# An attention-and-MLP kernel: feed-forward over four stages at once in its second half, and one order list for the whole program

## The chip, the core and the metric

The kernel runs on one core of a Trainium2 chip. The metric is device time in microseconds (us) of one execution; the median of several runs is given.

## The reference

A linear attention with decay over `r`, `k`, `v` of 4 batches, 8 heads, 768 tokens and 48 channels, then a feed-forward layer over all 3072 tokens of 384 channels:

```python
for t in range(S):
    cur = np.einsum('bhd,bhe->bhde', u[None] * kt, vt)
    y[:, :, t] = np.einsum('bhd,bhde->bhe', rt, state + cur)
    state = w[None, :, :, None] * state + np.einsum('bhd,bhe->bhde', kt, vt)
...
x = attn_out.transpose(0, 2, 1, 3).reshape(B * S, H * D)     # 3072 x 384
h = x @ w_in                                                 # 384 x 2048
g = np.maximum(0.01 * h, h)
return g @ w_out                                             # 2048 x 384, float32
```

## The kernel before

The work is cut into 24 stages of 128 tokens of one batch; stage n is chunk n // 4 of batch n % 4, so that the state that stage n leaves is wanted by stage n + 4. Inside a stage the recurrence is turned into matrix products. Everything is kept in bf16, with sums in PSUM, which has eight banks that are taken and given back in the order of the program.

What a stage needs, with the letters by which the order list names each step (the number behind the letter is the stage):

- `r`, `k`, `v`: its three loads, issued by GpSimd (line 220; 128 x 8 runs of 192 bytes each, cast to bf16 on the way). `wi`, `wo`: a quarter of `w_in` and of `w_out` (lines 230 and 234), four of each, also GpSimd's.
- `P`: VectorE multiplies r (`Pnq`) or k (`Pnk`) by a table of decay powers into `qk` (line 361). `T` and `t`: TensorE transposes the one or the other and ScalarE (with `@` VectorE) copies it out to `tp`, in stages 0 to 5; from stage 6 on `XnT`, a DMA transpose issued by SyncE (line 366), does it. For stage 0 the raw r and k are cast (`c0q`, `c0k`, ScalarE), transposed, and multiplied by the tables on VectorE (`t0q`, `t0k`); `E` makes these tables with four exponentials on ScalarE.
- `A`: eight small matmuls of 48 rows on TensorE (`a_mm`, line 453), q against k within the chunk, into two banks. `M`: VectorE masks each of the two (`Mna`, `Mnb`; line 462, from stage 4 on a predicated copy, line 466) into `at`.
- The term in u: in stages 0 to 3 `X`, `D`, `Q` (a product on VectorE, four small matmuls, a scaling of v on VectorE). From stage 4 on `q` (`row_sums`): three VectorE instructions, `ku` (line 390), `rku` (line 392) and a reduction (line 394), and `Q` (`diag_tile`): two GpSimd multiplies (line 401) that lay these sums on the diagonal of `at`, before the masks are copied over it.
- `Y`: 16 or 28 matmuls on strips of 32 columns of TensorE's array (`y_mm`, line 592), `y`: ScalarE copies the result to `xT`.
- `K`: four matmuls for the state (`kv_mm`, line 494), `S`: VectorE folds them in (`state`; an add from PSUM, line 560, and a multiply by the decay, line 562; one instruction in stages 0 to 3).
- The feed-forward layer: `G` and `g`, first product for one stage and four blocks of 128 hidden channels (12 matmuls of 128 columns, line 631) and its leaky ReLU on ScalarE into `gT`; `J` and `j`, the same for a pair of stages and two blocks (6 matmuls of 256 columns, line 654). `H` and `h`: second product of one stage (16 matmuls of 384 columns, line 678), its copy on ScalarE and its store from SyncE's queue.
- `F`: fillings, matmuls of ones by ones whose result nobody reads (line 267). `v0z` and `v0y` zero the gap columns of `v_sb` for stages 0 to 3 and 4 to 23 (line 285). `utab`, `qtab`, `ktab`, `Cu`, `Cw`, `Wl`, `W`, `C`: small tables.

Each engine carries out its instructions strictly in the order in which the program lists them; a scheduler class adds the semaphores. Up to stage 5 of the feed-forward part (and up to stage 7 of the attention) the order is the list `ORDER`, written out by name. From there a loop over pairs m = 3 to 11 takes over: eight `g1_pair` with the `a_mm` of the next pair between or behind them, masks, preparation (`prep`, `row_sums`, `diag_tile`) of the pair after that, loads two pairs further, and around `y_part`, `kv_mm` and `state` the two `g2` of the pair before. These loads are paced: each waits until TensorE has done the second `g1_pair` of its m. `xT` and `gT` have three buffers of two stages.

Of the kernel before, what the change touches and what calls it, by code (L numbers as in the profile page):

```python
# [26 lines left out]
ORDER = """
w8 k0 r0 u8 u v0z v0 ones table v0y tcol trow r2 tri id wlz id8 k2 zr F18 Cw c0k Wl wi1 F4 T0k qk0 E r5 c0q F10 T0q wu8
k1 F1 TQ t0k r1 TK t0q qtab Cu ktab P2q v2 F3 A0 X0 W C P2k T2q k3 M0a D0 T2k t2q Q0 v1 t2k M0b F16 A2 r3 X2 Y0 P1k M2a
wi3 D2 y0 T1k P1q M2b v3 t1k F3 T1q K2 u16 Q2 G0.1 k5 S2 t1q Y2 g0.1 P3k k4 X1 A1 y2 P5q K1 P3q D1 T3k wi2 M1a T5q t3k  # L30
T3q U t5q@ r4 t3q G2.1 Q1 utab A3 wi0 X3 g2.1 G0.3 M1b wo0 M3b D3 K3 g0.3 Y1 v5 M3a G2.3 y1 Q3 k6 G1.3 P4k g2.3 q5 k7
Y3 g1.3 T4k y3 v4 G1.1 t4k S3 G3.2 wo1 g1.1 P4q P5k G3.1 Q5 g3.2 S1 T5k g3.1 T4q G3.3 q4 t4q G0.0 t5k r6 g3.3 A4 A5
g0.0 P0k G3.0 Q4 M5a K0 G1.2 g3.0 M5b S0 K5 G2.2 g1.2 wo3 G2.0 M4a g2.2 wo2 P7k G1.0 g2.0 P6k M4b r7 K4 Y5 g1.0 S4 Y4
r9 y5 G0.2 S5 y4 k9 J2.7 g0.2 q6 r8 J2.5 j2.7 J2.6 k8 j2.5 J2.4 P6q j2.6 Q6 J2.0 X6T j2.4 J2.1 j2.0 J2.2 j2.1 k10 H2
j2.2 P7q q7 v6 X7T v7 P9q v8 H3 P9k h2 q9 X9T Q7 P8q H1 h3 Q9 q8 v9 P8k A6 h1 X8T A7 M6b H0 Q8 M6a M7b M7a v11 K7 Y6 h0
r10 S7 Y7 y6 K6 k11 y7 J2.3 S6 v10 j2.3 r11
"""
# [89 lines left out]
def bass_rwkv5_eagle__then__act_leaky_relu_kernel(  # L127
# [317 lines left out]
    def a_mm(n):  # L445
        it = n % NTP
        at_bank[n] = (take(), take())

        def emit():
            for p in range(NP):  # L450
                for hh in range(2):
                    rows = slice(64 * hh, 64 * hh + D)
                    last = PE.matmul(at_bank[n][hh][0][:, 128 * p:128 * p + 128], tp[it][rows, NP + p, :],  # L453
                                     tp[it][rows, p, :], start=True, stop=True)
# [167 lines left out]
    def g1(n, grp):
        ps_g, key = g_bank[n, grp] = take()
        m, half = divmod(n, 2)
        ix, t = m % NX, slice(128 * half, 128 * half + 128)
# [9 lines left out]
        add("pe", emit, R=[("xT", ix, half), ("win", grp)], W=[key, ("pace", n, grp)])

    def g1_out(n, grp):
        ps_g, key = g_bank[n, grp]
        m, half = divmod(n, 2)
        ig, t = m % NG, slice(128 * half, 128 * half + 128)  # L640
        add("act", lambda: A.activation(gT[ig][:, 4 * grp:4 * grp + 4, t],  # L641
                                        ps_g[:, :].rearrange("p (f t) -> p f t", t=128), AF.Prelu, alpha=0.01),
            R=[key], W=[("gT", ig, half, 2 * grp), ("gT", ig, half, 2 * grp + 1)])
        give(key)

    def g1_pair(m, j):
        ps_g, key = g_bank[m, j, 2] = take()
        ix = m % NX

        def emit():  # L650
            for f in range(2):
                fb = 2 * j + f
                for s in range(NSL):
                    last = PE.matmul(ps_g[:, 256 * f:256 * f + 256], w_in_sb[:, s, 128 * fb:128 * fb + 128],  # L654
                                     xT[ix][:, s, :], start=s == 0, stop=s == NSL - 1)
            return last

        add("pe", emit, R=[("xT", ix, 0), ("xT", ix, 1), ("win", j // 2)],
            W=[key, ("pace", 2 * m, j), ("pace", 2 * m + 1, j)])

    def g1_pair_out(m, j):
        ps_g, key = g_bank[m, j, 2]
        ig = m % NG
        add("act", lambda: A.activation(gT[ig][:, 2 * j:2 * j + 2, :].rearrange("p f t -> p (f t)"),  # L664
                                        ps_g[:, :], AF.Prelu, alpha=0.01),
            R=[key], W=[("gT", ig, 0, j), ("gT", ig, 1, j)])
# [4 lines left out]
    def g2(n, c0=0, c1=HD):
        ps_o, key = o_bank[n, c0] = take()
        m, half = divmod(n, 2)
        ig = m % NG

        def emit():
            for s in range(NFB):
                last = PE.matmul(ps_o[:, 0:c1 - c0], gT[ig][:, s, 128 * half:128 * half + 128], w_out_sb[:, s, c0:c1],  # L678
                                 start=s == 0, stop=s == NFB - 1)
# [47 lines left out]
    for name in ORDER.split():  # L727
        if name in single:
            single[name]()
        else:  # L730
            what, n, rest = re.match(r"([A-Za-z]+?)(\d+)(.*)$", name).groups()
            stage[what](int(n), rest)
    for m in range(FIRST // 2, NST // 2):
        due, ahead, far = ([n for n in (2 * m + x, 2 * m + x + 1) if n < NST] for x in (2, 4, 6))
        late = m < FIRST // 2 + LATE
        for j in range(8):
            if j == VISIT and not late:
                for n in due:
                    a_mm(n)
            g1_pair(m, j)  # L740
            g1_pair_out(m, j)
        for n in due if late else ():
            a_mm(n)
        if not late:
            for n in ahead:
                prep(n)
        for n in due:
            a_mask(n)
        if late:
            for n in ahead:  # L750
                prep(n)
        for n in far:
            load_stage(n, pace=[("pace", 2 * m, 1)])
        for n in ahead:
            row_sums(n)
            diag_tile(n)
        g2(2 * m - 2)
        g2_out(2 * m - 2)
        for n in due:
            y_part(n)  # L760
        turning = [n for n in due if n < NST - NB]
        for n in turning:
            kv_mm(n)
        for n in turning:
            state(n)
        g2(2 * m - 1)
        g2_out(2 * m - 1)
    g2(NST - 2)
    g2_out(NST - 2)
# [60 lines left out]
```

## Time and profile before

| what | us |
|---|---|
| median of 3 runs | 169.99 (169.92 to 170.53) |
| the profiled execution | 170.09 |
| its span in the profile | 168.3 |
| TensorE matmuls busy in the span | 161.6 |
| VectorE busy | 110.2 |
| GpSimd busy | 111.1 |
| ScalarE busy | 91.0 |

Busy times are sums over the span. The granted TensorE clock is 1.00 in every 10 us of the span but the last, where it is 0.99. In listings of groups the columns are line, engine, operation, output and inputs, shape, count, then busy us and mean ns of one, then the idle time just before and what ended it. PE is TensorE, PEld its weight loads, DVE VectorE, ACT ScalarE, POOL GpSimd, SP SyncE.

### The profile page before, as it was taken

What the parts mean: (1) busy time and instruction counts of PE and PEld (TensorE: products, weight loads), DVE (VectorE), ACT (ScalarE), POOL (GpSimd) and SP (SyncE); (2) the same over time, 40 slices, a digit from 0 to 9 for tenths busy, and PEclk for the clock granted to TensorE, in tenths of its full rate; (3) what the DMA queues carried; (4) which work ended last, traced back from release to release, by engine and by line L of the source; (5) the groups of instructions that cost most, each with busy time, mean ns of one, the idle gap of its engine ahead of it and who ended that gap; (6) DMA issues with size and microseconds to landing.
All of it is one profiled execution on the core that took longest, in us unless ns stands there. A gap on an engine that the chain in (4) does not pass through costs nothing.

```text
span 168.3 us, 4915 instructions
## 1 busy us (share of the span) xinstructions
PE 161.6 (96%) x2116; PEld 122.6 (73%) x2116; DVE 110.2 (66%) x221; ACT 91.0 (54%) x168; POOL 111.1 (66%) x125
## 2 busy tenths in 40 slices
PE   5889979999999999999999999999999999999994
PEld 5767869986568768768668768768678678668663
DVE  7499978828992497497599998996996805000000
ACT  4658777892228537537436536537537447449221
POOL 7999996999699929939939976975960540000000
PEclk9999999999999999999999999999999999999999
DMA  7999999999999996995994995994999111011012
GB/s 108 105 157 162 171 192 167 150 170 155 150 230 150 118 95 186 80 126 156 90 147 129 125 162 142 153 97 113 146 104 143 32 47 51 0 51 47 29 65 95
DMA packets 101263, 20.18 MB, mean 120 GB/s; under 512 B 94457, under 2 KB 101242, under 8 KB 101242
## 3 DMA queue, kind: packets, MB, share of 16 engines
q0 software_dynamic: 76512, 10.03, 93.3%
q1 hardware_dynamic: 23690, 9.64, 28.1%
q8 instruction: 16, 0.26, 0.7%
q10 hardware_dynamic: 1040, 0.20, 0.6%
q14 instruction: 5, 0.04, 0.1%
HBM read 20.45 MB, written 4.72 MB: 150 GB/s over the span
## 4 chain that ended last, share of the span: by engine, by line
PE 69%; POOL 12%; DMA 9%; DVE 7%; issue 1%; ACT 0%; POOLq 0%; DVEq 0%
PE ps L678 31%; PE ps L654 29%; DMA k_sb<-in_k_dram 5%; PE ps L592 5%; DMA r_sb<-in_r_dram 4%; POOL r_sb L220 3%; DVE qk L361 3%; PE ps L453 3%; POOL k_sb L220 3%; POOL v_sb L220 2%; PE ps L494 2%; DVE at L466 1%; POOL at L401 1%; POOL w_in_sb L230 1%; DVE rku L392 1%; DVE ku L390 1%
## 5 line engine op out<-in xcount | busy, mean ns | idle before, releaser
L678 PE MATMUL ps<-w_out_sb,gT 128*128 128x384 bf16 (+2 forms) x400 | 65.6, 320 | 0.0
L401 POOL TENSOR_TENSOR at<-ident,s_tok 128x512 bf16<-128x512 bf16 x40 | 42.8, 1101 | 21.0 <-DVE s_tok L394 21.0
L654 PE MATMUL ps<-xT,w_in_sb 128*128 128x256 bf16 x480 | 54.9, 273 | 0.0
L678 PEld LDWEIGHTS ps<-w_out_sb,gT 128*128 128x128 bf16 x400 | 37.7, 98 | 22.4
L664 ACT ACTIVATE gT<-ps 128x512 bf16<-128x512 f32 x80 | 47.8, 597 | 8.7 <-PE ps L654 4.0
L654 PEld LDWEIGHTS ps<-xT,w_in_sb 128*128 128x128 bf16 x480 | 46.4, 98 | 6.7
L690 ACT ACTIVATE out_sb<-ps 128x384 f32<-128x384 f32 (+2 forms) x25 | 12.0, 479 | 55.8 <-PE ps L678 55.8
L466 DVE CAST_PREDICATED at<-mask,ps 128x512 bf16<-128x512 uint16 x40 | 25.0, 684 | 21.8 <-PE ps L453 21.8
L220 POOL DMA_DIRECT2D k_sb<-in_k_dram x23 | 21.1, 923 | 3.3 <-PE ps L654 3.3
L220 POOL DMA_DIRECT2D v_sb<-in_v_dram x24 | 22.2, 925 | 0.8 <-POOLq L815 0.8
L220 POOL DMA_DIRECT2D r_sb<-in_r_dram x23 | 21.0, 914 | 0.0
L392 DVE TENSOR_TENSOR rku<-r_sb,ku 128x384 bf16<-128x384 bf16 x20 | 17.8, 892 | 0.7
L631 PE MATMUL ps<-xT,w_in_sb 128*128 128x128 bf16 x192 | 12.6, 219 | 0.5 <-DMA w_in_sb<-in_moe_w_in_dram 0.5
L606 ACT ACTIVATE xT<-ps 128x384 bf16<-128x384 f32 x24 | 10.9, 491 | 2.3 <-PE ps L592 2.2
L361 DVE TENSOR_TENSOR qk<-r_sb,qtab 128x384 bf16<-128x384 bf16 x23 | 9.1, 400 | 4.5 <-DMA r_sb<-in_r_dram 4.1
L631 PEld LDWEIGHTS ps<-xT,w_in_sb 128*128 128x128 bf16 x192 | 10.9, 98 | 1.3 <-DMA w_in_sb<-in_moe_w_in_dram 0.7
L394 DVE TENSOR_REDUCE s_tok<-rku 128x8 f32<-128x384 bf16 x20 | 11.1, 553 | 0.7
L641 ACT ACTIVATE gT<-ps 128x512 bf16<-128x512 f32 x16 | 9.5, 599 | 3.4 <-PE ps L631 2.9
L562 DVE TENSOR_TENSOR st<-sum_t,wl 128x384 bf16<-128x384 bf16 x16 | 10.7, 672 | 0.5
L592 PE MATMUL ps<-at,v_sb 128*32 128x128 bf16 x384 | 10.7, 219 | 0.0
L361 DVE TENSOR_TENSOR qk<-k_sb,ktab 128x384 bf16<-128x384 bf16 x23 | 9.9, 434 | 0.7 <-DMA k_sb<-in_k_dram 0.7
L592 PEld LDWEIGHTS ps<-tp,st 128*32 128x32 bf16 x240 | 7.2, 96 | 3.1 <-issue 2.5
(64 smaller groups left out, 120.9 us busy)
## 6 DMA issues: line engine op xcount, KB each, us to landing
out_dram<-out_sb SPq DMA_DIRECT2D x23, 192.0 KB, 2.2
v_sb<-in_v_dram POOLq DMA_DIRECT2D x24, 96.0 KB, 5.3
r_sb<-in_r_dram POOLq DMA_DIRECT2D x23, 96.0 KB, 5.4
k_sb<-in_k_dram POOLq DMA_DIRECT2D x23, 96.0 KB, 5.1
w_in_sb<-in_moe_w_in_dram POOLq DMA_DIRECT2D x4, 384.0 KB, 7.0
w_out_sb<-in_moe_w_out_dram POOLq DMA_DIRECT2D x4, 384.0 KB, 8.5
tp<-qk SPq DMA_TRANSPOSE x18, 4.1
k_f<-in_k_dram ACTq DMA_DIRECT2D x1, 192.0 KB, 2.8
```

The costliest lines, as they stand in the source:

```text
L220: add("pool", lambda: G.dma_start(dst, src), R=pace, W=[(which, n)], dma=f"{which}{n}")
L361: add("dve", lambda: V.tensor_tensor(qk[iq][:, H * half:H * half + H, 0:D], hd(src), hd(tab[:, :]), ALU.mult), R=[(name, n), "qk"[half] + ...
L392: add("dve", lambda: V.tensor_tensor(rku[i2][:, :], r_of(n), ku[i2][:, :], ALU.mult), R=[("r", n), ("ku", i2)], W=[("rku", i2)])
L394: add("dve", lambda: V.tensor_reduce(s_tok[i2][:, :], hd(rku[i2][:, :]), AX.X, ALU.add), R=[("rku", i2)], W=[("s", i2)])
L401: add("pool", lambda hh=hh, s_of=s_of: G.tensor_tensor(at[ia][:, hh, :, :], ident[:, :].unsqueeze(1).to_broadcast([128, NP, 128]), s_of.un ...
L466: add("dve", lambda: V.copy_predicated(at[n % NAT][:, hh, :, :], mask[:, :].bitcast(mybir.dt.uint16).unsqueeze(1).to_broadcast([128, NP, 1 ...
L592: last = PE.matmul(ps_y[32 * q:32 * q + 32, 128 * s:128 * s + 128], a, m, start=not whole and step == 0, stop=step == len(columns[q]) - 1)
L631: last = PE.matmul(ps_g[:, 128 * f:128 * f + 128], w_in_sb[:, s, 128 * fb:128 * fb + 128], xT[ix][:, s, t], start=s == 0, stop=s == NSL - 1)
L654: last = PE.matmul(ps_g[:, 256 * f:256 * f + 256], w_in_sb[:, s, 128 * fb:128 * fb + 128], xT[ix][:, s, :], start=s == 0, stop=s == NSL - 1)
L664: add("act", lambda: A.activation(gT[ig][:, 2 * j:2 * j + 2, :].rearrange("p f t -> p (f t)"), ps_g[:, :], AF.Prelu, alpha=0.01), R=[key], ...
L678: last = PE.matmul(ps_o[:, 0:c1 - c0], gT[ig][:, s, 128 * half:128 * half + 128], w_out_sb[:, s, c0:c1], start=s == 0, stop=s == NFB - 1)
L690: add("act", lambda: A.activation(out_sb[io][:, c0:c1], ps_o[:, 0:c1 - c0], AF.Copy), R=[key], W=held)
```

## The change

From stage 12 on, the first product is done for four stages and one block of hidden channels at a time: `Z` and `z`, three matmuls of 512 columns and one copy of 128 x 512. One function `g1_wide` with its width stands for `G`, `J` and `Z`. `xT` and `gT` become two buffers of four stages. The loop over pairs is gone; the list names every step of all 24 stages but the last `H`, which is still done in two halves behind it. No load waits for a place of TensorE any more: GpSimd issues each as it comes to it in the list. Fillings are F10, F20 and F2, 32 matmuls, where there were F18, F4, F10, F1, F3, F16 and F3, 55 matmuls.

```diff
-FIRST, NB, PACE = 6, B, 3
-TURNED, DIAG, CARRY, EXACT, RAW, VISIT, LATE = 6, 4, 4, 1, 1, 3, 3
+NB = B
+TURNED, DIAG, CARRY, EXACT, RAW = 6, 4, 4, 1, 1
 ORDER = """
-w8 k0 r0 u8 u v0z v0 ones table v0y tcol trow r2 tri id wlz id8 k2 zr F18 Cw c0k Wl wi1 F4 T0k qk0 E r5 c0q F10 T0q wu8
-k1 F1 TQ t0k r1 TK t0q qtab Cu ktab P2q v2 F3 A0 X0 W C P2k T2q k3 M0a D0 T2k t2q Q0 v1 t2k M0b F16 A2 r3 X2 Y0 P1k M2a
...
+w8 trow k0 table ones wlz wi1 r0 zr u v0z F10 tcol id u8 id8 tri c0k r2 k2 c0q r3 k1 qk0 wu8 Cw Wl r1 E F20 T0q t0q T0k
+t0k W TQ qtab P2q TK ktab k3 Cu C v0 P2k A0 M0a T2q u16 t2q P3q v2 X0 v3 wi3 P1k k4 M0b P1q v1 T2k U t2k T3q k5 utab
+T1k t1k X2 A2 P3k r4 r5 D0 M2a Q0 T1q t1q wi2 t3q T3k t3k F2 A1 D2 M2b Y0 wi0 y0 A3 K2 Q2 Y2 M1b G0.1 wo2 X3 D3 v4 X1
+D1 y2 v5 M3a G2.1 g2.1 M3b G0.3 Q3 Y3 y3 M1a G2.3 Q1 Y1 y1 g2.3 wo3 g0.3 G3.3 g3.3 P0k S2 P4k K0 G1.1 wo0 g0.1 r7 q5 k7
+T4k t4k G3.1 P5k T5k g1.1 K1 S0 q4 G3.2 g3.2 t5k wo1 G0.2 S1 G1.3 Q4 P4q g0.2 T4q t4q P5q T5q Q5 v0y k6 t5q@ g1.3 G2.2
+r6 G0.0 k9 g2.2 A4 r9 A5 G1.0 g3.1 M4a M4b k8 g1.0 M5a K3 G1.2 K5 r10 g1.2 v6 k10 G3.0 g3.0 Y4 y4 M5b Y5 G2.0 y5 J2.6
+J2.0 g0.0 g2.0 J2.3 J2.1 j2.1 J2.4 S5 P7k J2.7 j2.4 j2.7 j2.6 r8 S3 v7 P7q j2.3 j2.0 q7 v8 Q7 K4 S4 J2.2 j2.2 J2.5 P6k
+k11 X7T v9 H3 P6q q6 Q6 r11 H1 r13 H0 P8k k12 q9 Q9 r12 A7 j2.5 P9k k14 r15 X6T h0 A6 M6b M6a P9q X9T M7a H2 K7 Y6 v12
+y6 M7b Y7 r14 y7 H4 J3.1 P8q X8T q10 q8 J3.6 k13 h4 h3 P10k h1 J3.2 h2 q11 j3.2 J3.7 j3.1 k15 S7 K6 S6 J3.4 J3.0 j3.6
+j3.7 A9 M9b v11 A8 J3.3 j3.3 K8 P11k S8 H5 Q8 v10 M8a M8b Y8 y8 Q11 M9a Y9 y9 J3.5 J4.0 j4.0 P11q X11T j3.4 j3.0 J4.4
+j3.5 j4.4 k17 J4.3 j4.3 P12k J4.6 P10q X10T q12 h5 J4.7 v13 P12q P13q P13k J4.2 q13 K9 Q10 q14 K12 j4.2 r16 X13T j4.7
+Q14 J4.5 j4.5 S12 P14q Q13 K11 P15k Q12 P15q S11 J4.1 S9 X12T H6 q15 Q15 A10 P14k A11 M11a j4.1 H7 X14T v15 M11b M10b
+j4.6 K13 k19 X15T v14 M10a Y11 y11 Y10 y10 h6 A13 M13b r22 M13a H8 P16q h7 h8 k23 A14 M14a A12 M12b A15 H9 M12a M14b
+K10 M15a J5.5 j5.5 S10 M15b J5.6 Y14 y14 Y12 Y15 P19k r17 q17 Y13 y15 J5.4 v17 v16 J5.0 y12 y13 Z3.14 k16 K14 j5.6 J5.3
+P17q S13 j5.4 P16k J5.7 S14 Z3.9 P17k r19 X17T K17 Z3.0 P19q j5.3 X19T r21 k18 P21q j5.7 r18 P18k z3.14 Z3.15 z3.9 v18
+q16 k21 v19 j5.0 Z3.13 z3.13 P18q Q16 K18 S18 J5.2 j5.2 z3.15 Z3.8 Z3.7 k20 q18 K15 X16T z3.8 P21k K16 Z3.11 S16 Q17
+q19 Q19 h9 J5.1 Z3.1 Z3.12 r20 j5.1 H10 X21T z3.7 z3.12 z3.11 A17 z3.0 q21 S17 M17a S15 A16 M16a Z3.2 z3.2 H11 M16b
+z3.1 M17b X18T v22 k22 A18 Q18 h10 A19 M18a Q21 M18b A21 Z3.10 Z3.6 z3.10 M19a Y16 P22q y16 r23 Y18 M19b y18 Y17 Y19
+y17 P20q v20 K19 S19 y19 Z3.4 v23 z3.4 Z3.3 z3.3 Z4.9 Z3.5 z3.6 Z4.8 z4.8 z4.9 Z4.12 q22 Q22 Z4.1 Z4.7 z3.5 P23q q23
+M21b v21 Z4.11 h11 Z4.15 P22k P20k X20T Z4.5 z4.15 q20 Z4.10 H14 X22T P23k X23T z4.12 Z4.2 M21a z4.1 z4.7 z4.10 Z4.3
+z4.5 z4.2 H13 z4.3 A23 Q23 A20 h14 A22 z4.11 M23a M23b M22a Z4.4 H12 Q20 M20b M20a Y20 Y21 M22b h12 Y22 y22 Y23 y23 H15
+z4.4 y21 y20 Z5.12 Z5.1 z5.1 Z5.7 Z5.2 Z5.0 Z4.13 z5.0 Z5.5 h15 z5.5 Z5.13 Z5.15 z4.13 z5.2 z5.7 Z4.14 z5.15 Z4.0 z4.0
+z4.14 Z5.11 z5.13 Z5.8 Z4.6 z4.6 h13 Z5.10 Z5.3 H18 z5.10 z5.12 Z5.6 z5.6 H16 Z5.9 h16 z5.3 h18 z5.11 Z5.4 H17 h17 z5.8
+Z5.14 z5.14 H19 z5.9 z5.4 H21 H20 h20 H22 h19 h22 h21
 """
...
-    NQK, NTP, NVS, NAT, NT, NX, NG, NO = 6, 6, 6, 6, 10, 3, 3, 4
+    NQK, NTP, NVS, NAT, NT, NX, NG, NO = 6, 6, 6, 6, 10, 2, 2, 4
...
-    xT = [SB(f"xT{i}", [128, NSL, 256]) for i in range(NX)]
-    gT = [SB(f"gT{i}", [128, NFB, 256]) for i in range(NG)]
+    xT = [SB(f"xT{i}", [128, NSL, 512]) for i in range(NX)]
+    gT = [SB(f"gT{i}", [128, NFB, 512]) for i in range(NG)]
...
+    def g1_wide(n0, width, fb0, count):
+        ps_g, key = g_bank[n0, width, fb0] = take()
+        ix, slots = n0 // 4 % NX, range(n0 % 4, n0 % 4 + width)
+        t, step = slice(128 * slots[0], 128 * slots[0] + 128 * width), 128 * width
+
+        def emit():
+            for f in range(count):
+                fb = fb0 + f
                 for s in range(NSL):
+                    last = PE.matmul(ps_g[:, step * f:step * f + step], w_in_sb[:, s, 128 * fb:128 * fb + 128],
                                      xT[ix][:, s, t], start=s == 0, stop=s == NSL - 1)
             return last
...
+        "G": lambda n, x: g1_wide(n, 1, 4 * int(x[1:]), 4), "g": lambda n, x: g1_wide_out(n, 1, 4 * int(x[1:]), 4),
+        "J": lambda n, x: g1_wide(2 * n, 2, 2 * int(x[1:]), 2), "j": lambda n, x: g1_wide_out(2 * n, 2, 2 * int(x[1:]), 2),
+        "Z": lambda n, x: g1_wide(4 * n, 4, int(x[1:]), 1), "z": lambda n, x: g1_wide_out(4 * n, 4, int(x[1:]), 1),
...
-        "L": lambda n, x: load_stage(n, pace=[("pace", PACE, 0)]),
+        "L": lambda n, x: load_stage(n),
...
-    for m in range(FIRST // 2, NST // 2):
...
+    run(ORDER)
```

More of the change, by code (lines that the diff above doesn't have):

```diff
@@ L23 @@
 NSL = HD // 128
-FIRST, NB, PACE = 6, B, 3
-TURNED, DIAG, CARRY, EXACT, RAW, VISIT, LATE = 6, 4, 4, 1, 1, 3, 3
+NB = B
+TURNED, DIAG, CARRY, EXACT, RAW = 6, 4, 4, 1, 1
 ORDER = """
-w8 k0 r0 u8 u v0z v0 ones table v0y tcol trow r2 tri id wlz id8 k2 zr F18 Cw c0k Wl wi1 F4 T0k qk0 E r5 c0q F10 T0q wu8
-k1 F1 TQ t0k r1 TK t0q qtab Cu ktab P2q v2 F3 A0 X0 W C P2k T2q k3 M0a D0 T2k t2q Q0 v1 t2k M0b F16 A2 r3 X2 Y0 P1k M2a
-wi3 D2 y0 T1k P1q M2b v3 t1k F3 T1q K2 u16 Q2 G0.1 k5 S2 t1q Y2 g0.1 P3k k4 X1 A1 y2 P5q K1 P3q D1 T3k wi2 M1a T5q t3k
@@ L31 @@
[L31 to L35, printed above, removed]
@@ L36 @@
-r10 S7 Y7 y6 K6 k11 y7 J2.3 S6 v10 j2.3 r11
+w8 trow k0 table ones wlz wi1 r0 zr u v0z F10 tcol id u8 id8 tri c0k r2 k2 c0q r3 k1 qk0 wu8 Cw Wl r1 E F20 T0q t0q T0k
+t0k W TQ qtab P2q TK ktab k3 Cu C v0 P2k A0 M0a T2q u16 t2q P3q v2 X0 v3 wi3 P1k k4 M0b P1q v1 T2k U t2k T3q k5 utab
+T1k t1k X2 A2 P3k r4 r5 D0 M2a Q0 T1q t1q wi2 t3q T3k t3k F2 A1 D2 M2b Y0 wi0 y0 A3 K2 Q2 Y2 M1b G0.1 wo2 X3 D3 v4 X1
+D1 y2 v5 M3a G2.1 g2.1 M3b G0.3 Q3 Y3 y3 M1a G2.3 Q1 Y1 y1 g2.3 wo3 g0.3 G3.3 g3.3 P0k S2 P4k K0 G1.1 wo0 g0.1 r7 q5 k7
@@ L604, in y_out @@
         ps_y, key = y_bank[n]
-        m, half = divmod(n, 2)
-        add("act", lambda: A.activation(xT[m % NX][:, :, 128 * half:128 * half + 128],
+        ix, slot = n // 4 % NX, n % 4
+        add("act", lambda: A.activation(xT[ix][:, :, 128 * slot:128 * slot + 128],
                                         ps_y[:, 0:HD].rearrange("p (s t) -> p s t", t=128), AF.Copy),
-            R=[key], W=[("xT", m % NX, half)])
+            R=[key], W=[("xT", ix, slot)])
         give(key)
@@ L620, in bass_rwkv5_eagle__then__act_leaky_relu_kernel @@
     g_bank = {}
[L622 to L625, printed above, removed]
+    def g1_wide(n0, width, fb0, count):
+        ps_g, key = g_bank[n0, width, fb0] = take()
+        ix, slots = n0 // 4 % NX, range(n0 % 4, n0 % 4 + width)
+        t, step = slice(128 * slots[0], 128 * slots[0] + 128 * width), 128 * width
         def emit():
-            for f in range(4):
-                fb = 4 * grp + f
+            for f in range(count):
+                fb = fb0 + f
@@ L630, in emit @@
                 for s in range(NSL):
-                    last = PE.matmul(ps_g[:, 128 * f:128 * f + 128], w_in_sb[:, s, 128 * fb:128 * fb + 128],
+                    last = PE.matmul(ps_g[:, step * f:step * f + step], w_in_sb[:, s, 128 * fb:128 * fb + 128],
                                      xT[ix][:, s, t], start=s == 0, stop=s == NSL - 1)
             return last
[L635 to L666, printed above, removed]
+        add("pe", emit, R=[("xT", ix, slot) for slot in slots] + [("win", fb0 // 4)],
+            W=[key] + [("pace", n0 + i, fb0) for i in range(width)])
+    def g1_wide_out(n0, width, fb0, count):
+        ps_g, key = g_bank[n0, width, fb0]
+        ig, slots = n0 // 4 % NG, range(n0 % 4, n0 % 4 + width)
+        t = slice(128 * slots[0], 128 * slots[0] + 128 * width)
+        add("act", lambda: A.activation(gT[ig][:, fb0:fb0 + count, t],
+                                        ps_g[:, :].rearrange("p (f t) -> p f t", t=128 * width), AF.Prelu, alpha=0.01),
+            R=[key], W=[("gT", ig, slot, fb0 + f) for slot in slots for f in range(count)])
@@ L672, in g2 @@
         ps_o, key = o_bank[n, c0] = take()
-        m, half = divmod(n, 2)
-        ig = m % NG
+        ig, slot = n // 4 % NG, n % 4
         def emit():
             for s in range(NFB):
-                last = PE.matmul(ps_o[:, 0:c1 - c0], gT[ig][:, s, 128 * half:128 * half + 128], w_out_sb[:, s, c0:c1],
+                last = PE.matmul(ps_o[:, 0:c1 - c0], gT[ig][:, s, 128 * slot:128 * slot + 128], w_out_sb[:, s, c0:c1],
                                  start=s == 0, stop=s == NFB - 1)
             return last
-        add("pe", emit, R=[("gT", ig, half, j) for j in range(8)] + [("wout", i) for i in range(4)], W=[key])
+        add("pe", emit, R=[("gT", ig, slot, fb) for fb in range(NFB)] + [("wout", i) for i in range(4)], W=[key])
     def g2_out(n, c0=0, c1=HD):
@@ L718, in bass_rwkv5_eagle__then__act_leaky_relu_kernel @@
         "Y": lambda n, x: y_sum(n), "y": lambda n, x: y_out(n), "K": lambda n, x: kv_mm(n), "S": lambda n, x: state(n),
-        "G": lambda n, x: g1(n, int(x[1:])), "g": lambda n, x: g1_out(n, int(x[1:])),
-        "J": lambda n, x: g1_pair(n, int(x[1:])), "j": lambda n, x: g1_pair_out(n, int(x[1:])),
+        "G": lambda n, x: g1_wide(n, 1, 4 * int(x[1:]), 4), "g": lambda n, x: g1_wide_out(n, 1, 4 * int(x[1:]), 4),
+        "J": lambda n, x: g1_wide(2 * n, 2, 2 * int(x[1:]), 2), "j": lambda n, x: g1_wide_out(2 * n, 2, 2 * int(x[1:]), 2),
+        "Z": lambda n, x: g1_wide(4 * n, 4, int(x[1:]), 1), "z": lambda n, x: g1_wide_out(4 * n, 4, int(x[1:]), 1),
         "H": lambda n, x: g2(n), "h": lambda n, x: g2_out(n), "F": lambda n, x: fill(n),
-        "L": lambda n, x: load_stage(n, pace=[("pace", PACE, 0)]),
+        "L": lambda n, x: load_stage(n),
         "r": lambda n, x: load_first(n, "r") if n < EXACT else load_one(n, "r"),
@@ L726, in bass_rwkv5_eagle__then__act_leaky_relu_kernel, with run @@
     }
[L727 to L732, printed above, removed]
-    for m in range(FIRST // 2, NST // 2):
[L734 to L769, printed above, removed]
+    def run(names):
+        for name in names.split():
+            if name in single:
+                single[name]()
+            else:
+                what, n, rest = re.match(r"([A-Za-z]+?)(\d+)(.*)$", name).groups()
+                stage[what](int(n), rest)
+    run(ORDER)
     for c0, c1 in ((0, 256), (256, HD)):
```

## The prediction

> **What bounds the kernel now.** First the busy line and the slices of the page: is an engine full, and when?
>
> ```profile
> PE 161.6 (96%) x2116; PEld 122.6 (73%) x2116; DVE 110.2 (66%) x221; ACT 91.0 (54%) x168; POOL 111.1 (66%) x125
> ...
> PE   5889979999999999999999999999999999999994
> ...
> DVE  7499978828992497497599998996996805000000
> ...
> POOL 7999996999699929939939976975960540000000
> ```
>
> TensorE falls short only in the first six slices (to 25 us) and in the last. Then the chain of waits in order of time (start, length, what), for what the full stretch is made of:
>
> ```profile
> 126.05 1.97 PE ps L654 x18
> 128.02 0.55 PE ps L453 x16
> 128.57 3.38 PE ps L654 x30
> 131.95 2.60 PE ps L678 x16
> ...
> 155.50 10.45 PE ps L678 x80
> 165.95 0.02 issue
> 165.97 0.28 ACT out_sb L690
> ```
>
> From 49.9 us to the end it is TensorE alone, back to back. The chain gives prices: a 384-column matmul costs 2.60/16 = 162.5 ns, a 256-column one 1.97/18 = 109.2 ns, `a_mm` 0.28, and the `y_mm` and `kv_mm` rows of the same view 0.45 and 0.22 each. The time lies in the first 25 us and in whatever would open a gap later. So I ask what feeds TensorE, VectorE, by groups kept apart by shape (busy us, mean ns | idle before):
>
> ```profile
> L401 POOL TENSOR_TENSOR at<-ident,s_tok 128x512 bf16<-128x512 bf16 x40 | 42.8, 1101 | 21.0 <-DVE s_tok L394 21.0
> ...
> L392 DVE TENSOR_TENSOR rku<-r_sb,ku 128x384 bf16<-128x384 bf16 x20 | 17.8, 892 | 0.7
> ...
> L562 DVE TENSOR_TENSOR st<-sum_t,wl 128x384 bf16<-128x384 bf16 x16 | 10.7, 672 | 0.5
> ```
>
> The same multiply of 128x384 bf16 costs 892 ns here, 672 there, and 358 at its quickest. The timeline says why:
>
> ```profile
> 61.98 4.32 POOL L401 TENSOR_TENSOR at<-ident,s_tok 128x512 bf16<-128x512 bf16 x4 [3.07 <-DVE s_tok L394]
> ```
>
> ```profile
> 61.81 0.35 DVE L390 TENSOR_TENSOR ku<-k_sb,u_tab 128x384 bf16<-128x384 bf16 x1
> 62.20 1.08 DVE L392 TENSOR_TENSOR rku<-r_sb,ku 128x384 bf16<-128x384 bf16 x1
> 63.31 0.55 DVE L394 TENSOR_REDUCE s_tok<-rku 128x8 f32<-128x384 bf16 x1
> 63.78 0.55 DVE L560 TENSOR_TENSOR sum_t<-ps,st 128x384 bf16<-128x384 f32 x1
> 64.36 1.03 DVE L562 TENSOR_TENSOR st<-sum_t,wl 128x384 bf16<-128x384 bf16 x1
> ```
>
> While GpSimd multiplies a diagonal tile (two of 1.1 us for a stage), a VectorE multiply with both inputs in SBUF ends only after GpSimd's instruction does; one that reads PSUM (L560, and the masks L466 with 684 ns throughout) runs on. Over all: L392 20 x 0.53 us, L562 16 x 0.31, and some 3.9 on L361 and L390, 19.6 us in 20 tiles: **one us of VectorE for each diagonal tile**. In the loop of before nothing is late by it, as VectorE has that time to spare.
>
> **The change part by part.** The profiled execution took 170.09 us, 168.3 of them the span, 0.1 over the median of 169.99; what lies around it I leave alone.
>
> Wide matmuls: for stages 12 to 23, 288 matmuls of 256 columns (31.45 us) become 144 of 512. From 256 to 384 columns the rows rise by 53.3 ns in 128, so I estimate 215.8 ns and 31.08 us: **-0.4**. Bounds for one: 162.5 ns (the 384 row) and 218.4 (two of 256), -8.0 to 0. The Trainium skill's page TensorE: Matmul & The Clock Gate, section Back-to-back issue gap, gives some 131 ns for N=512 in a real kernel, which would make it -12.6; its isolated formula gives 215.8. The rows at 256 and 384 follow the isolated one.
>
> Fewer fillings: 32 instead of 55. They stand before 13.4 us, between waits for VectorE; the 1.3 us of issue turns into waiting: **0**, at best -1.3. Should the array's clock be granted later without them, only a few transposes and `a_mm` of under 0.4 us each before 11 us run at twice the price, and VectorE is later than these: 0 to +0.5.
>
> Fewer crossings: each step from long matmuls into `a_mm` or `y_mm` costs 0.1 us of draining (a matmul row of 0.655 becomes 0.751). 18 groups become 14: **-0.4**.
>
> Start, to the first `g1_wide` of two stages: VectorE's list decides. From t0q to P5q stand 2 turn-outs (1.38 us), 10 quick P (3.6) and P0k (0.55), C (0.35), 8 masks (5.48), 4 X (1.68), 4 Q (2.18), 3 S (1.65), q5 and q4 (2.6): 19.5 us. It starts at 6.8, when E's four exponentials end, as the cast c0q now stands ahead of them (before: 6.26). k2 is later, since wi1 (1.9 us of queue) and r2 stand ahead of it: landings in the trace of before come 0.72 us apart for a tile, 1.9 for a weight block; k2 at 9.7 makes P2k wait 0.7. So q4 ends at 25.8, and Q4's two GpSimd multiplies start just there, ahead of P4q and P5q: both are held, P5q ends near 28.2. After it TensorE has T5q, six G, A4, A5, K3, K5, Y4, Y5: 0.23 + 4.1 + 0.55 + 0.4 + 0.9 = 6.2, first J at 34.4. Before had done the same work at 32.8: **+1.5** (rounded down for gaps in my waits; -0.3 without any wait, +3.6 if v0y, 1.12 us, moved from 1.5 us to behind P5q, is held as well: else A4 and the G ahead of A5 cover it). Loads are unpaced now and GpSimd lists the k and r of stages 6 to 10 earlier; nothing waits for them in my sums.
>
> Y8, Y9 and J4.0: after K8 VectorE has S8 and three masks, 0.45 + 0.91 + 2.05 = 3.4, TensorE H5 and Y8 3.05; then J4.0 has only J3.5 to hide y9: **+0.7** (0.3 to 1.2).
>
> Y11 and Y10: from M9a's end, where Y9 starts, VectorE's list to M10a has ten P (3.6), q12 to q15 (5.2), S12, S11, S9 (2.7), four masks (2.7): 14.3 us unhindered. TensorE has Y9, nine J (5.9), K9, K12, K11, K13, H6, H7, A10, A11, Y11, 13.3, and the 0.3 wait: due at 13.7. Already 0.6 late, and the tiles Q10, Q14, Q13, Q12 all fall in it, each at one us: 4.6 late; I take **+3.5**, as one may fall beside masks (0.4 to 5.5).
>
> H11: it takes the PSUM bank that M17a frees. From K16, TensorE has 6.6 us to it; VectorE S16, q19, q21, S17, M17a, 5.6 with its start. Two tiles (Q17, Q19) fall in it: **+1.0** (0 to 3). Behind: the short waits for a copy at H9, Z3.14, Y19, H21, where a list step follows its releaser by 0.1 to 0.25 us too little: **+0.3** (0 to 1). A23 and Y20 to Y23 keep over 3 us: 0.
>
> ScalarE's copies are as many columns in as many instructions (597 ns for 512), 0; `gT` and `xT` in two buffers of four stages hold as much as three of two and more, and each Z out waits only for H long done: 0.
>
> Sum: -0.4 - 0.4 + 1.5 + 0.7 + 3.5 + 1.0 + 0.3 = +6.2; 170.09 + 6.2, less the 0.1 to the median, is **176.2 us**.
>
> **The rivals.** (1) The list holds: GpSimd's tiles fall beside masks and reductions, or earlier; the unhindered sums above are all within 0.7 us of what TensorE needs, which reads like a list drawn up with VectorE's quick prices. Then -0.8 with 0.6 for Y10, 0.3 for the start, 0.5 for Y8 to J4.0 and the rest: 170.6, between 169.2 and 171.5. For it: the multiplies are held only if they meet. Against: 19.6 us of holding in before.
>
> (2) Faster: the start. TensorE before loses 0.66 us at 22.3 to wi2, 0.66 at 24.3 to P5k, behind r4, which landed at 23.1, and 0.5 at 45 to 50. In the new list r4 lands near 20. If VectorE is not held, P5q ends by 26.3 and the first J stands at 32.5; -0.3 -0.5 -0.8 gives 168.4. It decides at P5q: before 26.5 the start gains. Against: VectorE's own 19.5 us fill that time.
>
> (3) GpSimd is late: seven unpaced loads stand between Q9 and Q8, 0.87 us each; Q8 ends near 59 where M8a wants it near 61.5. At the 1.06 us that the first issue takes, 29 loads give 5.5 us more, 3 late at Y8, and again at Y10: 180.
>
> (4) Wide matmuls at the 384 row's price: 144 x 53 ns less, 7.7 us, all on the path: 168.5 beside my waits. The page's 131 ns is this rival's stronger form.
>
> **How the numbers follow.** Held VectorE: 0.62, its own range 172.5 to 180. List holds: 0.15. Faster start: 0.13. GpSimd late: 0.07. Wide matmuls cheap: 0.03. A change under 0.5% (0.85 us) is what a measurement of this kernel hardly tells from none: below 169.15 lie (2), (4) and a little of (1), 0.16; between, most of (1), 0.11; above, 0.73. The range reaches down into (1) and (2) to 168.8, up to 180.0.
>
> **What would show it.** Right: groups L392 and L562 of the new profile with means well over 892 and 672 ns, or as many held in 60 to 85 us; TensorE idle before L592 near 75 to 83 us, put down to masks at L466; a first 256-column matmul near 34.5; 512-column ones 216 ns apart. Wrong: TensorE back to back from 33 us on, or 512-column matmuls at 165 ns, or long idle time of VectorE before L466 put down to GpSimd's `at`.

## The result and the profile after

| | before | after |
|---|---|---|
| median, us | 169.95 (169.66 to 170.53, 4 runs) | 180.95 (179.89 to 181.31, 4 runs) |
| profiled execution, us | 170.09 | 181.27 |
| its span, us | 168.3 | 179.5 |

The ratio is 1.063, with a 95% interval of 1.058 to 1.069: the new list is 11 us slower. The forecast was slower, at 176.2, with 180.0 as the end of its range. Line numbers have moved: `qk` is L378, `ku` L407, `rku` L409, `diag_tile` L418, the masks L483, `a_mm` L470, `kv_mm` L511, `state` L577 and L579, `g1_wide` L648, `g2` L672.

The page first, the busy line and the slices (4.5 us each):

```profile
PE 165.9 (92%) x1949; PEld 111.0 (62%) x1949; DVE 115.4 (64%) x221; ACT 83.1 (46%) x168; POOL 111.2 (62%) x125
...
PE   5999999999999799689999938799999999999994
...
DVE  5497888859799999996687999979908000000000
...
POOL 8999969999999981969992929965630000000000
PEclk9999999999999999969999999999999999999999
```

TensorE is now open in three places far behind the start: 58 to 63 us, 72 to 81 and 103 to 117. At the second of them the clock row drops too. (Its 9 in the first slices stands where nothing is recorded: the first record of a granted clock of 1.0 is at 19.5 us, and matmuls of 128 columns are 107 ns apart before it and 56 behind it.) The groups that VectorE's multiplies form (kept apart by shape) say what has grown:

```profile
L407 DVE TENSOR_TENSOR ku<-k_sb,u_tab 128x384 bf16<-128x384 bf16 x20 | 14.6, 729 | 0.0
L579 DVE TENSOR_TENSOR st<-sum_t,wl 128x384 bf16<-128x384 bf16 x16 | 12.7, 796 | 0.5
L378 DVE TENSOR_TENSOR qk<-r_sb,qtab 128x384 bf16<-128x384 bf16 x23 | 12.2, 543 | 0.2 <-DMA r_sb<-in_r_dram 0.2
...
L409 DVE TENSOR_TENSOR rku<-r_sb,ku 128x384 bf16<-128x384 bf16 x20 | 9.3, 466 | 0.7
```

Against the quick price of each (350 ns for `qk` and `ku`, 358 for `rku` and `st`), with `qk` from k at 495, that is 24.5 us of holding, where before had 19.6. It has also moved: off `rku` (892 before), onto `ku` (392 before) and `st` (672 before). The waits of TensorE name the line that came last:

```profile
PE ps L648 <- DVE sum_t L577: 3.0, 1, 3.0
PE ps L470 <- DVE sum_t L577: 2.4, 2, 1.5
PE ps L470 <- DVE at L483: 1.1, 3, 0.7
```

None of the long ones is TensorE waiting for an operand that a mask writes. `sum_t` is the add of `state` that reads the PSUM bank of `kv_mm` and so gives it back: TensorE stands because the next bank is not free. The timeline of the second opening shows how that comes about:

```profile
71.20 6.62 POOL L418 TENSOR_TENSOR at<-ident,s_tok 128x512 bf16<-128x512 bf16 x6 [4.38 <-PE ps L648]
71.53 0.92 DVE L579 TENSOR_TENSOR st<-sum_t,wl 128x384 bf16<-128x384 bf16 x1
72.37 1.19 DVE L378 TENSOR_TENSOR qk<-r_sb,qtab 128x384 bf16<-128x384 bf16 x1
73.49 1.19 DVE L378 TENSOR_TENSOR qk<-k_sb,ktab 128x384 bf16<-128x384 bf16 x1
74.61 1.19 DVE L378 TENSOR_TENSOR qk<-r_sb,qtab 128x384 bf16<-128x384 bf16 x1
75.72 0.54 DVE L577 TENSOR_TENSOR sum_t<-ps,st 128x384 bf16<-128x384 f32 x1
...
76.32 0.40 PE L470 MATMUL ps<-tp 48*128 48x128 bf16 x8 [1.48 <-DVE sum_t L577]
...
77.44 4.46 PE L672 MATMUL ps<-w_out_sb,gT 128*128 128x384 bf16 x16 [0.72 <-DVE sum_t L577]
```

Three tiles (Q14, Q13, Q12) run back to back for 6.6 us. Each VectorE multiply with both inputs in SBUF ends with one of GpSimd's six; the add from PSUM at 75.72 takes its usual 0.54. That add is S11, and A11 waits 1.5 us for its bank; S9 behind it is what H7 waits for. Then the last row: the 16 matmuls of H7 take 4.46 us where the same row costs 2.76 elsewhere in this view. The granted clock is 0.5 for 3.4 us from 77.5 us on. The Trainium skill's page TensorE: Matmul & The Clock Gate, Part 1, has the clock decided in windows of about 3.4 us, and the length of this stretch agrees.

### The profile page after: what moved, and what is told of

The parts are those of the page before. It is cut to its first block, busy times and chain, and to the rows that moved or that the text cites. A ratio compares the mean times of both kernels' runs of the same rounds, so it can differ in the third digit from the quotient of the medians.

```text
span 179.5 us, 4576 instructions
## 1 busy us (share of the span) xinstructions
PE 165.9 (92%) x1949; PEld 111.0 (62%) x1949; DVE 115.4 (64%) x221; ACT 83.1 (46%) x168; POOL 111.2 (62%) x125
## 4 chain that ended last, share of the span: by engine, by line
PE 65%; DVE 26%; DMA 3%; issue 3%; POOL 1%; ACT 0%; DVEq 0%; POOLq 0%
PE ps L672 27%; PE ps L648 26%; DVE qk L378 6%; DVE st L579 5%; PE ps L609 5%; DVE at L483 4%; DVE ku L407 3%; DMA k_sb<-in_k_dram 3%; PE ps L470 3%; DVE sum_t L577 3%; DVE rku L409 3%; DVE s_tok L411 2%; PE ps L441 2%; PE ps L511 1%; PE ps L602 1%
## 5 line engine op out<-in xcount | busy, mean ns | idle before, releaser
L648 PE MATMUL ps<-xT,w_in_sb 128*128 128x128 bf16 (+2 forms) x528 | 69.9, 286 | 3.3 <-DVE sum_t L577 3.0
L659 ACT ACTIVATE gT<-ps 128x512 bf16<-128x512 f32 x96 | 52.2, 605 | 38.8 <-PE ps L648 38.4
L672 PE MATMUL ps<-w_out_sb,gT 128*128 128x384 bf16 (+2 forms) x400 | 67.2, 325 | 1.7 <-DVE at L483 1.0
L648 PEld LDWEIGHTS ps<-xT,w_in_sb 128*128 128x128 bf16 x528 | 43.6, 100 | 21.0 <-DVE sum_t L577 3.3
L672 PEld LDWEIGHTS ps<-w_out_sb,gT 128*128 128x128 bf16 x400 | 38.5, 99 | 27.9 <-issue 1.7
L418 POOL TENSOR_TENSOR at<-ident,s_tok 128x512 bf16<-128x512 bf16 x40 | 42.9, 1101 | 19.9 <-DVE s_tok L411 15.4
L483 DVE CAST_PREDICATED at<-mask,ps 128x512 bf16<-128x512 uint16 x40 | 25.2, 682 | 9.2 <-PE ps L470 9.2
L407 DVE TENSOR_TENSOR ku<-k_sb,u_tab 128x384 bf16<-128x384 bf16 x20 | 14.6, 729 | 0.0
L579 DVE TENSOR_TENSOR st<-sum_t,wl 128x384 bf16<-128x384 bf16 x16 | 12.7, 796 | 0.5
L470 PE MATMUL ps<-tp 48*128 48x128 bf16 x192 | 9.2, 232 | 3.6 <-DVE sum_t L577 2.4
L378 DVE TENSOR_TENSOR qk<-r_sb,qtab 128x384 bf16<-128x384 bf16 x23 | 12.2, 543 | 0.2 <-DMA r_sb<-in_r_dram 0.2
L378 DVE TENSOR_TENSOR qk<-k_sb,ktab 128x384 bf16<-128x384 bf16 x23 | 11.3, 495 | 1.6 <-DMA k_sb<-in_k_dram 1.5
L577 DVE TENSOR_TENSOR sum_t<-ps,st 128x384 bf16<-128x384 f32 x16 | 8.8, 550 | 4.3 <-PE ps L511 4.3
L609 PE MATMUL ps<-at,v_sb 128*32 128x128 bf16 x384 | 10.9, 227 | 0.0
L470 PEld LDWEIGHTS ps<-tp 48*128 48x128 bf16 x192 | 5.9, 100 | 7.4 <-DVE sum_t L577 2.8
L409 DVE TENSOR_TENSOR rku<-r_sb,ku 128x384 bf16<-128x384 bf16 x20 | 9.3, 466 | 0.7
```

The lines of the kernel that those rows point to most:

```text
L378: add("dve", lambda: V.tensor_tensor(qk[iq][:, H * half:H * half + H, 0:D], hd(src), hd(tab[:, :]), ALU.mult), R=[(name, n), "qk"[half] + ...
L407: add("dve", lambda: V.tensor_tensor(ku[i2][:, :], k_of(n), u_tab[:, :], ALU.mult), R=[("k", n), "u_tab"], W=[("ku", i2)])
L418: add("pool", lambda hh=hh, s_of=s_of: G.tensor_tensor(at[ia][:, hh, :, :], ident[:, :].unsqueeze(1).to_broadcast([128, NP, 128]), s_of.un ...
L483: add("dve", lambda: V.copy_predicated(at[n % NAT][:, hh, :, :], mask[:, :].bitcast(mybir.dt.uint16).unsqueeze(1).to_broadcast([128, NP, 1 ...
L579: add("dve", lambda: V.tensor_tensor(new[:, :, :], sum_t[n % 4][:, :, :], wl[:, :, :], ALU.mult), R=[("sum", n % 4), "wl0", "wl1"], W=[("s ...
L609: last = PE.matmul(ps_y[32 * q:32 * q + 32, 128 * s:128 * s + 128], a, m, start=not whole and step == 0, stop=step == len(columns[q]) - 1)
```

## The experiments

First, is it the holding, and all of it? Which steps of TensorE were late can be summed from prices, but only a kernel without holding settles it. (Where an expectation names a loss "at" a step, the step behind it on TensorE is the one that waits; the text names that one.)

**e1_no_read**, the new kernel, in `diag_tile` (shortened):

```diff
-                at[ia][:, hh, :, :], ident[...], s_of..., ALU.mult), R=["ident", ("s", n % 4)], W=[("at", ia, hh)])
+            add("pool", lambda: G.iota(spare[:, :], ...), R=["spare"], W=["spare"])        # 128 x 448, writes only
+            add("pool", lambda hh=hh: G.memset(at[ia][:, hh, :, :], 0.0), R=[("s", n % 4)], W=[("at", ia, hh)])
```

> The changed kernel, with GpSimd's two multiplies per diagonal tile replaced by two pairs that only write (an iota into a spare tile and a memset of the half of `at`), of about the same length; the term in u of stages 4 to 23 is left out. Theory (VectorE is held by GpSimd's tiles): rows ku, rku, st and qk fall to 350 to 360 ns each, TensorE's losses between 57 and 117 us (11 us in the changed kernel) shrink to under 3, the time is 170 to 173 us. Rival (the list simply puts too much VectorE work ahead of masks and state, held or not): the same rows get quicker, but the waits at A10, H7 and Z3.1 stay above 6 us in sum, the time is 177 or more. Rival (loads come too late without pacing): no change, 180 to 181.

Measured: 169.66 us, ratio to before 0.9997 (0.9973 to 1.0022). The pair of write-only instructions takes 579 + 583 ns, a little more than the multiply's 1101, and GpSimd is nearly as busy in all (105.8 us, 111.2 in after). VectorE's groups are at their quick prices:

```profile
L408 DVE TENSOR_TENSOR ku<-k_sb,u_tab 128x384 bf16<-128x384 bf16 x20 | 7.0, 350 | 0.0
L578 DVE TENSOR_TENSOR st<-sum_t,wl 128x384 bf16<-128x384 bf16 x16 | 5.7, 358 | 0.6
```

All 11 us are gone: they are the holding and what follows from it. Without it the new list, wide matmuls and fewer fillings included, takes as long as the old one. The Trainium skill's page SBUF — State Buffer, section Who interferes with whom, says that a GpSimd operation contends with VectorE's two-input ones when it reads SBUF and not when it only writes; this run agrees (796 against 358 ns on `st`).

**e5_before_no_read**, the same edit in the kernel before:

> The kernel before, with the diagonal tiles made by instructions of GpSimd that only write (as in the first run; the term in u of stages 4 to 23 is left out). Theory (before is held just as often, but the loop leaves VectorE time to spare): rows rku and st fall from 892 and 672 ns to 358, VectorE's busy time by 15 to 20 us, and the time by no more than 0.8 us (the wait at Y6 and one at P of stages 8 and 9): 169.2 to 170. Rival (holding also costs before several us): 167 or less.

Measured: 169.66, ratio 1.0000 (0.9983 to 1.0016), with VectorE's busy time down from 110.2 to 91.3 us. So 19 us of holding in before cost nothing, and nearly 5 us more in after do not account for 11: what counts is which multiplies are held.

**e3_halves**, the new kernel with each 512-column matmul cut in two of 256 (shortened):

```diff
+                    for c in range(0, step, 256):
+                        w = min(step, 256)
+                        last = PE.matmul(ps_g[:, step * f + c:step * f + c + w], ..., xT[ix][:, s, a:a + w], ...)
```

> The changed kernel with each 512-column matmul cut into two of 256 columns (288 instead of 144), same list, same copies, same buffers. Theory that width itself gives only the fixed part of a matmul: 109.2 ns each, +0.4 us, 181.3. Rival that 512 columns are worth more (cheaper than two of 256 by over 10 ns): +1.5 us or more. Rival that the wide form costs something: faster.

Measured: 180.57, ratio to before 1.065 (1.061 to 1.069), which is that of after. The wide matmul is worth next to nothing; the price of one is read from the end of after's chain of waits, where nothing else interferes:

```profile
156.29 0.65 PE ps L648 x3
156.93 2.60 PE ps L672 x16
159.53 1.29 PE ps L648 x6
```

That is 216 ns for 512 columns, the estimate of the prediction.

**e6_before_few**, the kernel before with F10, F20 and F2 in place of its seven fillings:

> The kernel before with 32 fillings where the new list has them (F10 at the start, F20 ahead of the first transposes of stage 0, F2 for the F16). Theory of the clock: granted later than 7.6 us, up to 20; the transposes, a_mm and strips before it at half speed, first 256-column matmul 0.3 to 1.2 us later than 32.99; 170.3 to 171.2. Rival (fillings stand only in waits and the clock comes by itself): within 0.2 us of before.

Measured: 170.91, ratio 1.0057 (1.0031 to 1.0083). The granted clock is 1.0 from 7.1 to 10.5 us, 0.5 to 17.3 and 1.0 from there, where before has 1.0 from 7.6 us on, and the first step `J` comes at 33.82 instead of 32.99. In the kernel before the fillings that were left out are worth 1 us.

**e2_fill**, the new kernel with F18, F4, F20, F3, F8 and F2 (55 matmuls):

```diff
-... zr u v0z F10 tcol ... wu8 Cw Wl r1 E F20 ... k3 Cu C v0 ... T2k U t2k ...
+... zr u v0z F18 tcol ... wu8 Cw F4 Wl r1 E F20 ... k3 Cu F3 C v0 ... T2k F8 U t2k ...
```

> The changed kernel with 55 fillings again (F18, F4, F20, F3, F8, F2). Theory that the missing fillings delay the array's clock: granted from 8 us instead of 19.5, first 256-column matmul 0.5 to 1.2 us earlier than 33.7, the time 179.8 to 180.5 us. Rival that VectorE alone sets the start: clock earlier, first 256-column matmul unchanged within 0.2 us, the time 181. Rival that fillings stand in the way of real work: later.

Measured: 181.36, ratio 1.065 (1.059 to 1.070): no gain, though the clock is granted from 4.6 us on and VectorE reaches P4q 2.2 us earlier (23.36 for 25.58). The gain ran into the tiles of stages 5 and 4:

```profile
23.36 4.67 DVE L378 TENSOR_TENSOR qk<-r_sb,qtab 128x384 bf16<-128x384 bf16 x2
23.37 4.17 POOL L418 TENSOR_TENSOR at<-ident,s_tok 128x512 bf16<-128x512 bf16 x4
```

P4q and P5q now start together with Q4 and Q5 and last 4.67 us for the two; T4q waits 3.1 us for them, the clock halves for 3.4 us from 28.5, and the first `J` is at 35.9 where after had 33.73. A second such stretch follows the wait at Z3.1, at 107.0 us. In after the same two start 0.54 us behind the first of the four multiplies and last 1.84 us together.

**e7_start**, e2_fill with the products put ahead of the row sums whose tiles held them:

```diff
-... P0k S2 P4k K0 G1.1 ... q4 ... Q4 P4q g0.2 T4q t4q P5q T5q Q5 ... (P5k behind G3.1)
+... P0k S2 P4k P4q P5k P5q K0 G1.1 ... q4 ... Q4 g0.2 T4q t4q T5q Q5 ...
```

> The changed kernel with 55 fillings and P4q, P5k, P5q moved ahead of q5 and q4, so that no product with both inputs in SBUF stands behind the start of GpSimd's tiles Q4 and Q5. Theory (with the clock early VectorE is earlier by over 2 us, and what took it back when only the fillings were restored was P4q and P5q, held 4.2 us by Q4 and Q5): first 256-column matmul at 31 to 32.3 instead of 33.7 and 35.9, the time 178 to 179.5 with the later waits as they were. Rival (PSUM banks or loads set the start): 33 or later, 181.

Measured: 179.02, ratio 1.052 (1.048 to 1.057). The first `J` is at 30.75 us, 2.0 ahead of before for equal work, the clock is full from 6.7 us and is never lost. Against after, 3.0 us are won at the start and 1.7 as H7 runs at the full clock; 1.1 are lost at A6 to a DMA transpose and 1.1 at `y_mm` to masks, which H7 had covered. The waits at A8, H5, A11, H7, Z3.1, H11 and from A18 to A21 stand as they were (8.4 us in the list of TensorE's waits, 8.2 in after). In sum that is the 2.4 us between the two profiled executions (181.27 and 178.92).

**e4_order**, the new kernel with the tiles of the late places moved beside masks and matmuls that don't need VectorE:

```diff
- S7 ... q12 ... q13 K9 Q10 q14 ... Q14 ... Q13 ... Q12 ... q15 Q15 A10 ... q18 ... Q17 q19 ... q21 S17
+ (q13 Q13 q14 Q14 q15 Q15 behind M10a; Q12 behind Q10; Q17 behind v19; q18 behind S16; q21 behind M16b; S7 behind P8q)
```

> The changed kernel with the same instructions, but six list steps of VectorE and their GpSimd tiles moved: q13, q14, q15 behind the masks of stage 10, q18 behind S16, q21 behind M16b, S7 ahead of q10; Q12 and Q17 earlier. Theory (what is late is the masks and states that give PSUM banks back, behind sums that were in no hurry and were held): the waits at A10 to H7 fall from 4.1 us to under 1, at J5.1 and Z3.1 from 3.2 to under 0.5, the time 173 to 175.5 us. Rival that VectorE is short of time in the whole stretch, held wherever its work stands: waits move to Y12 to Y15 and to H11, the time 179 or more.

Measured: 177.66, ratio 1.043 (1.038 to 1.048): 3.3 us back, between the figures of the theory and the rival. Gone are the waits at A11 and H7, most of A8's, and Z3.1's goes from 3.0 to 0.4. New are A12, 1.2 us (a mask behind the moved row sums), the half clock behind it at H9, 1.7, and A21, 1.8 (the bank of M18, whose Q18 now stands behind loads).

**e8_beside**, both: e7_start with moves of this kind, chosen from the measured times of e4_order.

```diff
+ (q12 Q12 q13 Q13 behind P14k; q14 Q14 behind M10a; q15 Q15 behind M13a; Q10 behind Q11; q18 Q18 behind S16;
+  q21 behind M16b; Q17 behind v19; S7 behind P8q)
```

> As the run before, and in three later stretches the tiles put beside VectorE's masks, which read PSUM: Q10 behind Q11, q12 and q13 right ahead of the masks of stages 11 and 10, q14 and q15 between masks, Q17 ahead of Q16, q18 with Q18 behind S16, q21 behind M16b, S7 ahead of q10. Theory (what costs is not holding in sum but a product met by a tile where VectorE is due): TensorE's waits between 57 and 117 us under 2.5 us, the time 168.5 to 171.5. Rival (VectorE is too full there in any order): 174 or more, with TensorE waiting for masks at A14, A19 or Y14.

Measured: 177.63, ratio 1.041 (1.036 to 1.045). `st` is down to 502 ns and the holding to 18.7 us by the same count, less than in before. The time is the rival's all the same, but not by its masks: TensorE stands for other things:

```profile
PE ps L470 <- DMA tp<-qk: 3.6, 2, 2.7
PE ps L511 <- DVE qk L378: 2.7, 1, 2.7
```

```profile
74.34 4.16 POOL L418 TENSOR_TENSOR at<-ident,s_tok 128x512 bf16<-128x512 bf16 x4 [9.25 <-DVE s_tok L411]
```

With Q12 put later, GpSimd stands idle for 9.25 us ahead of it, and the loads listed behind it (v15 to k16) wait as well; 2.7 us of that come out at K17, behind a `qk` that waited for its k, with 3.4 us of half clock from 97.2 us behind them. This is the place of rival (3), GpSimd's queue, though with another cause than the one given there.

**e10_loads**, e8_beside with those loads put ahead of Q12:

```diff
- P14k q12 Q12 q13 Q13 ...
+ P14k v15 k19 v14 r17 k16 r19 r21 k18 r18 q12 Q12 q13 Q13 ...      (and Q7 behind P6q)
```

> The run with the tiles beside the masks, with nine loads (v15, k19, v14, r17, k16, r19, r21, k18, r18) moved ahead of Q12, where GpSimd stood idle from 65 to 74 us, and with Q7 behind P6q so that the two products that feed the transpose of stage 6 aren't held. Theory (the order of GpSimd's queue sets all that is left: holding where a tile runs beside a product, loads where a tile waits ahead of them): the waits of TensorE at Z3.9 (2.8 us and the half clock's 1.7 us behind it) and half of that at A7 (2.8) go: 172 us (170.5 to 174), the losses left being those at A9, J5.6 and Z3.15. Rival (four stages at once leave too few banks and buffers, whatever the order of loads and tiles): new waits of the same size elsewhere, 176.5 to 178.

Measured: 176.42, ratio 1.038 (1.034 to 1.042): the rival's value, though not by banks or buffers. The wait at K17 is gone; A6 keeps 1.5 us, and A14 and A15 now wait 1.3 and 2.2, with the half clock of H9 behind them (1.7), for another releaser:

```profile
PE ps L470 <- DMA tp<-qk: 5.0, 3, 2.2
```

Nine loads stand in GpSimd's queue in a row, and the four DMA transposes issued from 67.9 to 75.3 us land 7.3 to 10.5 us after their issue, where the first three from 96 us on, with few loads in the way, land after 2.8.

**e9_before_start**, the other way round: the kernel before with e7_start's list up to the first `J`, then its own.

> The kernel before with the start of the list of the run that put P4q, P5k and P5q ahead of q5 (with its 55 fillings), up to the last step ahead of the first J; the rest of its own list and its loop over pairs follow as they were. In that run the first J was at 30.75 us, against 32.77 for equal work in the kernel before. If the start of the new list is worth something by itself and all that is lost comes later, 168.0 us (167.3 to 168.8), the 2.0 us less. If something later in the kernel before sets its pace (GpSimd's loads, VectorE's products), the 2 us are given back by stage 10 and it reads 169.6 (within 0.4).

Measured: a ratio of 1.022 (1.018 to 1.027), slower than before, and by neither theory's figure. The six executions spread from 172.59 to 176.52. The profiled one took 175.62 and has 6.8 us of half clock from 51.8 us, which the quickest, with a mean granted clock of 1.00, can't have had; so I read its places and make no sum of it. The first `J` is at 31.21, 1.6 us earlier than in before, and then the loads are late:

```profile
33.06 0.36 DVE L361 TENSOR_TENSOR qk<-k_sb,ktab 128x384 bf16<-128x384 bf16 x1 [3.15 <-DMA k_sb<-in_k_dram]
35.78 0.36 DVE L361 TENSOR_TENSOR qk<-k_sb,ktab 128x384 bf16<-128x384 bf16 x1 [2.35 <-DMA k_sb<-in_k_dram]
```

VectorE loses 5.5 us to k7 and k6, S4 behind them gives its bank back 1.4 us late, and Y6 waits 2.4 us for masks that stand behind held products. The DMA row of before reads 9 in nearly every slice up to 63 us, so an earlier start finds its tiles not yet loaded; that loads quicker by bytes or runs would let it last wasn't tried. No version here beats the kernel before.

## Why the prediction was wrong, step by step

The direction and the mechanism were right, the size was not: 11.2 us in the span against 6.2. The lateness of TensorE (where a step ends, less the prices of all the steps up to it, in after against before) gives each term:

| term | predicted | measured |
|---|---|---|
| start, to the first `J`, fillings included | +1.5 | +1.0 |
| Y8, Y9, J4.0 | +0.7 | +1.7 |
| Y11, Y10 | +3.5 | +4.0 |
| H11 and all from K14 to A21, copies | +1.3 | +5.5 |
| crossings | -0.4 | -0.6 |
| wide matmuls | -0.4 | -0.4 |

**H11 is the term that failed**, mis-sized by a factor of four. It was worked out for one bank, M17a's, with two tiles, and what stands ahead of K16 was taken as free. The largest wait of the whole kernel lies there, 3.0 us at Z3.1. The rows of VectorE and GpSimd ahead of it, and the step that waits:

```profile
99.58 0.56 DVE L577 TENSOR_TENSOR sum_t<-ps,st 128x384 bf16<-128x384 f32 x1 [0.34 <-PE ps L511]
100.17 1.22 DVE L579 TENSOR_TENSOR st<-sum_t,wl 128x384 bf16<-128x384 bf16 x1
101.13 0.94 POOL L237 DMA_DIRECT2D k_sb<-in_k_dram  x1
101.32 3.05 DVE L407 TENSOR_TENSOR ku<-k_sb,u_tab 128x384 bf16<-128x384 bf16 x1
...
102.09 2.05 POOL L418 TENSOR_TENSOR at<-ident,s_tok 128x512 bf16<-128x512 bf16 x2
...
106.14 1.47 PE L648 MATMUL ps<-xT,w_in_sb 128*128 128x512 bf16 x6 [3.00 <-DVE sum_t L577]
```

At 99.58 VectorE still waits 0.34 us for TensorE, so it is on time there. Then a single `ku` lasts 3.05 us, held by both multiplies of Q16 and by 0.77 us ahead of the first of them, while GpSimd's row is still a load. The price of one us for a tile was a mean, and this one hold costs 2.7. K16's bank, given back by S16 behind it, was in no sum: the prediction took VectorE to be on time at K16 and counted from there. The other waits of this term are short: 0.6 us at H11 and 1.1 from A18 to A21, for masks.

**Y11 and Y10**: the sum said 4.6 late and 3.5 was taken; 4.0 came, but not as told, so that the size came near by luck. Some 2.2 us are banks (A11 and H7 wait for S11 and S9) and 1.7 us are H7 at half clock, under which the masks came in time: idle time before L609, named as the sign, is 0.2 us in all. In e3_halves and e7_start the clock held behind the same two waits, and the masks cost 1.1 us there instead. A half clock behind a wait was in no term.

**Fewer fillings at nothing** was wrong: +1.0 in e6_before_few, outside its bound of +0.5. The clock of 1.00 that the table of before has for the first 10 us hides what they do: its first record is at 7.6 us, and before 6 us the fillings stand 107 ns apart, behind 8.2 us 56. The total hid the error, as the **start** term, with the fillings in it, came out at +1.0 for +1.5: P4q and P5q were held for 1.2 us, not two, and P5q ended at 27.4, not 28.2. With the fillings back they were held for 4 (e2_fill), and the time was the same. The start is also not one number: with the same list up to there the first `J` is at 32.98 in e3_halves and 33.93 in e4_order, +0.2 to +1.2 from one execution to the next.

**Y8, Y9 and J4.0**: the `st` of S7 at 57.57, which lasts 1.84 us, puts S6 off, and A8 waits 1.0 us for its bank, ahead of the stretch that was summed. **Wide matmuls** and **crossings** were right; of the rivals, (4) is refuted by 216 ns, (1) and (2) by the losses above, (3) by VectorE's waits, none of which is for GpSimd's `at` and 1.7 us for loads in all of after. What of (2) is real is seen in e7_start and e9_before_start: the start can be 2 us earlier, and the loads don't allow it to last.

The signs asked for: 512-column matmuls 216 ns apart, right; `st` over 672, right, `rku` over 892, wrong (466, the holding moved to `ku`); the first 256-column matmul near 34.5, at 33.7; VectorE's long idle time put down to GpSimd's `at`, absent, as said.

## What to carry to other kernels

A list drawn up with quick prices is only as good as the meeting of VectorE's multiplies and GpSimd's: place GpSimd's reading instructions beside VectorE work that reads PSUM, and price every bank that VectorE has to give back, not only the operands it writes. Before crediting a shorter busy time or an earlier step, ask what is late next: here holding, then GpSimd's loads behind a waiting tile, then transposes behind the loads each took the place of the one removed. A wait of some 2 us on TensorE can bring a half clock with it, 1.7 us here, and a forecast needs a term for it that may come or not.
